# Moving blocks in and out of the inverse's layout: 32x32 transposes on VectorE in place of a trip through DRAM, and the first chunk inverted by itself

## The chip, the core and the metric

The kernel runs on one core of a Trainium2 chip. The core has a matrix engine (PE, TensorE; its weight loads are shown apart as PEld), a vector engine (DVE, VectorE), an activation engine (ACT, ScalarE), a general engine (POOL, GpSimd) and a sequencer for transfers (SP, SyncE). Each engine takes its instructions in the order of its own queue and waits on semaphores for the others. Transfers (DMA) are issued from the queues of SP, ACT and POOL. SBUF is the on-chip memory of 128 partitions, PSUM the accumulator memory that PE writes to. The metric is the device time of one execution in microseconds, as the median of several runs.

## The reference

A linear attention with the delta rule, and behind it a feed-forward block with LayerNorm. Four batches of eight heads, 768 tokens, head size 48; model width 384, hidden width 1536, all in fp32 (the feed-forward weights arrive as float64).

```python
k_n = k / (np.linalg.norm(k, axis=-1, keepdims=True) + 1e-06)
for t in range(S):
    y[:, :, t] = np.einsum('bhd,bhde->bhe', q[:, :, t], state)
    v_old = np.einsum('bhde,bhd->bhe', state, kt)
    state = state + bt[:, :, :, None] * np.einsum('bhd,bhe->bhde', kt, vt - v_old)
...
xn = (x - mu) / np.sqrt(var + 1e-06) * g_ln        # x: heads side by side, B x S x 384
ch = np.maximum(xn @ w_ch1, 0.0) @ w_ch2
return (x + ch)
```

## The kernel before, in words

The recurrence over tokens is cut into twelve chunks of C = 64 tokens. Inside a chunk the tokens' dependence on each other is a triangular system for each head. Its matrix comes from the Gram matrix K K^T of the chunk (64x64 for each of the 32 heads), scaled by beta and the norms. The kernel inverts that triangle, and then every chunk is a handful of matmuls: `recur` (L570) forms `p_k` and `p_y` from the running state, `p_u` with the inverse, the state's update `p_s`, and the output. The layout of the Gram matrices is: 64 tokens of one batch group on partitions 0 to 63, of the other group on 64 to 127, then 16 heads and 64 columns in the free dimension (`gsb`, 128 x 16 x 64).

The inverse (`inverse`, L443) works in another layout: one partition holds one diagonal block of one head, as L x L elements in its free dimension, so that DVE eliminates 128 blocks at once with L-1 pairs of small instructions (L475 multiplies, L480 subtracts). Chunks come in slabs of SLAB = 2. For the later slabs L is BK = 32: 2 chunks x 2 groups x 2 blocks x 16 heads are the 128 partitions (`blocks`, L402). For the first four chunks L is FB = 16 (`first_blocks`, L422), two chunks side by side in the free dimension. To get from one layout to the other, the kernel writes `gsb` to a DRAM tile `gd` (L389, L371), gathers blocks from there with eight or sixteen DMAs into `gb` (L406, L432), inverts, writes the result `xb` to a DRAM tile `xd` (L484), and scatters it with as many DMAs into `xt` (L414, L438), which has the Gram's layout again and was zeroed at the start (L258). After that `first_join` (L520) puts 16-blocks together to 32-blocks, and `join` (L492) 32-blocks to 64, each with a DVE transpose, two sets of small matmuls (`p_e`, `p_z`) and copies.

The feed-forward block of a chunk (`ffn`, L649) has 36 matmuls into `p_h`, evicted by ACT (`h_f`, L660), and 24 into `p_o`, evicted by DVE with the residual. Each matmul call leaves two records in the profile. The weights arrive as pairs of 32-bit words (float64) in twelve pieces of 768 KB into two buffers (`words`, L204) and are decoded to fp32 by `to_fp32` (L267): one ACT instruction (L277) and five DVE instructions (L279 to L294). Pieces 0 to 5 are the first matrix, 6 to 11 the second.

The order of the work: everything up to the `u` of chunk 0 stands in a block `in_this_order` (L686), which fixes the order of its instructions on each engine as written. The rest is written by a `Plan` (L24), whose due times (in units of its own) say in what order pieces are emitted; from there a scheduler gives each engine the earliest emitted instruction that it holds to be ready. `issue_after(ins)` keeps what is emitted within it behind `ins` on `ins`'s engine, and does not touch other engines. Before the change it is used with the last DVE instruction of the ordered block (`after`), for the weight pieces (L299) and the preparation of chunks 2 and 3, and in `queries` (L740) with the last gather on SP.

PSUM pools: `att` two buffers, `two` one buffer (shared by `p_g`, `p_k`, `p_u`, `p_s`), `by` one, `ffn` two (`p_h` and `p_o`).

Of the kernel before, what the change touches and what calls it, by code (L numbers as in the profile page):

```python
# [66 lines left out]

def in_turn(*gens):
    for gen in gens:
        yield from gen  # L70
# [3 lines left out]
def kernel(  # L74
# [10 lines left out]
):  # L85

# [29 lines left out]
    dram = ctx.enter_context(tc.tile_pool(name="dram", bufs=2, space=bass.MemoryType.DRAM))  # L116
# [94 lines left out]
    def places():  # L211

        for cc in range(SLAB):
            for e in range(2):
                for i in range(2):
                    yield ((cc * 2 + e) * 2 + i) * GH, cc, e, i
# [12 lines left out]
    with nc.allow_non_contiguous_dma(reason="short rows of g_ln"):  # L229
        load_beta_f(range(2), nc.gpsimd)  # L230
        nc.gpsimd.dma_start(out=g_sb, in_=g_ln.rearrange("(t p) -> p t", p=128))

# [10 lines left out]
    make_identity(nc, ident)  # L243
    umask = const.tile([128, 128], FP32, name="umask")
# [12 lines left out]
    for t in xts:  # L257
        nc.gpsimd.memset(t, 0.0)  # L258
# [40 lines left out]
    def weights(i0, i1, after=None, fetch=True):  # L299
        for i in range(i0, i1):  # L300
            with tc.issue_after(after) if after else nullcontext():
                to_fp32(i)
            if fetch:
                fetch_words()
            yield


    made, grams, deep_pools = {}, {}, []
    N_PREP = 4

    def turned(c, n):

        nc.vector.transpose(  # L313
            made[c][0][:, :, n].rearrange("p i (u t) -> p i u t", t=32), tblocks[(2 * c + n) % NTB]
        )

    def products(c, g, n0, n1):
# [10 lines left out]
        if n0 == 0:  # L328
            nc.scalar.copy(grams[c][0][:, heads].rearrange("p (j n) t -> p n j t", n=2), p_g[:, :, :, 0])  # L329
# [8 lines left out]

    def norms(c):
        ksum = work.tile([128, GH], FP32, name="ksum")  # L340
        for g in range(2):
            heads = slice(g * H, (g + 1) * H)
            ksq = work.tile([128, H, D], FP32, name="ksq", bufs=1)
# [12 lines left out]
    def new_chunk(c):  # L356
        gsb = work.tile([128, GH, C], FP32, name="gsb", bufs=4)
        gd = dram.tile([128, GH, C], FP32, name="gd", bufs=2 * SLAB)
        grams[c] = (gsb, gd)
# [3 lines left out]
    def prep(c):  # L363
# [7 lines left out]
        nc.sync.dma_start(out=grams[c][1], in_=grams[c][0])  # L371

    def prep_v(c):
# [3 lines left out]
        with tc.issue_after(after) if c < 4 else nullcontext():  # L377
            scale_v(c, norms(c), nc.gpsimd)
        yield

    def prep_g(c):

        new_chunk(c)
        with tc.issue_after(after) if c >= SLAB else nullcontext():
            turned(c, 0)
        for g in range(2):
            products(c, g, 0, 1)
            yield
        nc.sync.dma_start(out=grams[c][1], in_=grams[c][0])  # L389
# [10 lines left out]
    N_BLOCKS = 3 + BK // 2  # L400

    def blocks(m, engs):  # L402
        def gather(gb):
            for n, (p0, cc, e, i) in enumerate(places()):
                r0 = e * C + i * BK
                engs[n % len(engs)].dma_start(  # L406
                    out=gb[p0 : p0 + GH, 0],
                    in_=grams[SLAB * m + cc][1][r0 : r0 + BK, :, i * BK : (i + 1) * BK].rearrange("s h t -> h s t"),
                )

        def scatter(xd):
            for n, (p0, cc, e, i) in enumerate(places()):
                r0 = e * C + i * BK
                engs[n % len(engs)].dma_start(  # L414
                    out=xts[(SLAB * m + cc) % NXT][r0 : r0 + BK, :, i * BK : (i + 1) * BK],
                    in_=xd[p0 : p0 + GH, 0].rearrange("h s t -> s h t"),
                )
# [3 lines left out]
    def first_blocks(m, engs):  # L421

        def spots():
            for c in range(2):
                for e in range(2):
                    for b in range(C // FB):
                        p0 = (e * (C // FB) + b) * GH
                        yield p0, c, slice(e * C + b * FB, e * C + (b + 1) * FB), slice(b * FB, (b + 1) * FB)

        def gather(gb):  # L430
            for n, (p0, c, rows, cols) in enumerate(spots()):
                engs[n % len(engs)].dma_start(  # L432
                    out=gb[p0 : p0 + GH, c], in_=grams[SLAB * m + c][1][rows, :, cols].rearrange("s h t -> h s t")
                )

        def scatter(xd):
            for n, (p0, c, rows, cols) in enumerate(spots()):
                engs[n % len(engs)].dma_start(  # L438
                    out=xts[SLAB * m + c][rows, :, cols], in_=xd[p0 : p0 + GH, c].rearrange("h s t -> s h t")
                )  # L440

        return inverse(2, FB, beta_f[:, SLAB * m : SLAB * m + SLAB], gather, scatter)

    def inverse(nb, L, beta_l, gather, scatter):

        def square(pool, name, **kw):
            return pool.tile([128, BK * BK], FP32, name=name, **kw)[:, 0 : nb * L * L].rearrange(
                "p (b s t) -> p b s t", b=nb, s=L
            )
# [4 lines left out]
        gb = square(blk, "gb")  # L454
# [9 lines left out]
        xb = square(blk, "xb")  # L464
# [3 lines left out]
        nc.gpsimd.memset(xb, 0.0)  # L468
        nc.gpsimd.tensor_copy(out=diagonal(xb), in_=db)
# [13 lines left out]
        xd = square(dram, f"xd{L}")  # L483
        nc.sync.dma_start(out=xd, in_=xb)  # L484
        yield
        scatter(xd)
# [5 lines left out]
    def join(chunks):  # L492

        last = None
        for c in chunks:
            xt, gsb = xts[c % NXT], grams.pop(c)[0]
            xn = work.tile([128, GH, BK], FP32, name="xn", bufs=1)
# [22 lines left out]
    def first_join(c):  # L520

        xt, gsb = xts[c], grams[c][0]
        xn = blk.tile([128, GH, C], FP32, name="xn", tag="gb")
        nc.vector.transpose(xn, xt)
        quarters = [(slice(BK * n, BK * n + BK), BK * (n % 2)) for n in range(4)]
        p_e = ps_att([128, GH, FB], "p_e")
        for h in range(GH):
            for q, c0 in quarters:
                nc.tensor.matmul(p_e[q, h], gsb[q, h, c0 : c0 + BK], xn[q, h, c0 : c0 + FB])
        es = work.tile([128, GH, BK], FP32, name="es", bufs=1)[:, :, 0:FB]  # L530
        nc.scalar.mul(es, p_e, -1.0)
        yield
        p_z = ps_att([128, GH, FB], "p_z")
        for h in range(GH):
            for q, c0 in quarters:
                nc.tensor.matmul(p_z[q.start : q.start + FB, h], es[q, h], xt[q, h, c0 + FB : c0 + BK])
        for n, (q, c0) in enumerate(quarters):
            rows = slice(q.start, q.start + FB)
            copy = nc.vector.tensor_copy if n % 2 else nc.scalar.copy
            copy(out=xt[rows, :, c0 + FB : c0 + BK], in_=p_z[rows])  # L540
# [145 lines left out]
    with in_this_order(tc) as last:  # L686
        for c in two:
            for _ in prep_g(c):
                pass
        nc.vector.tensor_copy(out=scale_w[:, 0, 0:KC], in_=g_sb)  # L690
        nc.vector.tensor_scalar_mul(scale_w[:, 1, 0:KC], g_sb, 2.0**-52)
        for _ in weights(0, 1, fetch=False):
            pass
        inv = first_blocks(0, (nc.sync, nc.scalar))
# [4 lines left out]
        fetch_words()  # L699
        for _ in range(FB // 2):  # L700
            next(inv)
        knrm = norms(0)
        turned(0, 1)
        products(0, 0, 1, 2)
        for _ in inv:
            pass
        load_blocks(q, 1, 1, (nc.sync,))
# [116 lines left out]
```

## Time and profile before

| | |
|---|---|
| median of nine runs | 647.85 us (644.04 to 651.42) |
| the profiled execution's own time | 650.49 us |
| its span in the profile | 648.7 us |
| busy in the span: PE, DVE, ACT, POOL | 554.5, 328.6, 149.9, 124.0 us |
| DMA | 48.60 MB in 170980 packets, 164096 of them under 512 B |
| write of `gd`, one gather into `gb`, one scatter into `xt` (slabs of 32-blocks), issue to landing | 4.5, 3.5, 2.6 us |
| transfer of one piece of weights, 768 KB | 6.2 us |
| first FFN matmul (`p_h`) | at 90.6 us |

A line of a group of instructions reads: line of the kernel, engine, operation, written tile <- read tiles, shapes, count | busy us, mean ns of one | idle time of the engine just before them and what ended it. The chain of work that ended last is followed back from the end; its lines give start, length and what was running, "issue" being time for which the profile shows no wait. A waits line reads: who waited <- for whom: us in total, times, longest.

### The profile page before, as it was taken

To read this page: it belongs to the slowest core of one execution; us is meant where nothing else is said; L and a number is where in the kernel's file an instruction comes from. 1 tells how busy PE (TensorE), PEld (TensorE's weight loads), DVE (VectorE), ACT (ScalarE), POOL (GpSimd) and SP (SyncE) were. 2 spreads that over 40 slices of the span, in tenths; PEclk is the share of its full clock that TensorE was granted. 3 is DMA by queue.
4 is the path that set the end of the run, shared out by engine and by line. 5 is a ranking of instruction groups with operands and counts; after the bars stand their busy time and mean duration, and the time that the engine had idled before them with its cause. 6 is when DMAs were issued, how large, how long until landed. Compare 5 with 4: busy or idle time off the path is not lost.

```text
span 648.7 us, 19538 instructions
## 1 busy us (share of the span) xinstructions
PE 554.5 (85%) x8744; PEld 411.0 (63%) x8744; DVE 328.6 (51%) x683; ACT 149.9 (23%) x344; POOL 124.0 (19%) x197
## 2 busy tenths in 40 slices
PE   2016796875999979999989999799999799999997
PEld 2015684553786756786865877667868568777683
DVE  2453778998443994426982427953148722212000
ACT  2111332212231212232222221213312113213120
POOL 8042332015503222032310103020011000010100
PEclk9999998987999989899998999899999799999999
DMA  6775279547339304448215351141320020010101
GB/s 125 149 140 96 67 181 189 168 118 105 60 89 141 64 15 96 90 90 132 38 40 100 76 106 25 26 103 48 75 54 14 25 55 15 2 26 1 25 1 24
DMA packets 170980, 48.60 MB, mean 75 GB/s; under 512 B 164096, under 2 KB 165072, under 8 KB 170896
## 3 DMA queue, kind: packets, MB, share of 16 engines
q1 hardware_dynamic: 155760, 29.10, 24.5%
q0 software_dynamic: 6560, 17.72, 11.1%
q10 hardware_dynamic: 8576, 0.53, 0.9%
q8 instruction: 68, 1.11, 0.8%
q14 instruction: 16, 0.13, 0.1%
HBM read 33.69 MB, written 13.63 MB: 73 GB/s over the span
## 4 chain that ended last, share of the span: by engine, by line
PE 66%; DVE 12%; DMA 8%; issue 7%; ACT 3%; POOL 2%; SPq 2%; DVEq 0%; POOLq 0%; ACTq 0%
PE p_o L666 27%; PE p_h L655 22%; DVE tmp L475 4%; PE p_g L326 3%; DVE xb L480 3%; DMA words<-in_moe_w_ch_dram 3%; PE p_y L616 2%; PE p_e L504 2%; PE p_s L608 2%; DMA gb<-gd 2%; PE p_z L547 2%; DMA xt<-xd 2%; PE p_u L596 1%; DMA tb<-in_q_dram 1%; PE p_n L642 1%
## 5 line engine op out<-in xcount | busy, mean ns | idle before, releaser
L655 PE MATMUL p_h<-xnt,w_sb 128*128 128x256 f32 x864 | 213.6, 401 | 21.3 <-ACT h_f L660 14.9
L666 PE MATMUL p_o<-w_sb,h_f 128*128 128x384 f32 x576 | 200.6, 499 | 3.9 <-DVE w_sb L294 3.9
L655 PEld LDWEIGHTS p_h<-xnt,w_sb 128*128 128x128 f32 x864 | 166.4, 198 | 52.0 <-ACT h_f L660 17.7
L666 PEld LDWEIGHTS p_o<-w_sb,h_f 128*128 128x128 f32 x576 | 108.2, 193 | 71.1 <-DVE w_sb L294 4.2
L660 ACT ACTIVATE h_f<-p_h 128x256 f32<-128x256 f32 x144 | 54.7, 382 | 172.4 <-PE p_h L655 172.1
L326 PE MATMUL p_g<-kqt 48*64 48x64 f32 (+1 forms) x1024 | 36.1, 283 | 41.5 <-DVE kqt L313 35.0
L675 POOL DMA_DIRECT2D out_dram<-o x44 | 23.8, 544 | 249.0 <-DVE o L673 159.7
L148 POOL DMA_DIRECT2D tb<-in_k_dram x80 | 53.1, 670 | 74.8 <-DVE kqt L313 61.0
L326 PEld LDWEIGHTS p_g<-kqt 48*64 48x64 f32 x1024 | 28.1, 162 | 51.6 <-issue 33.3
L475 DVE TENSOR_TENSOR tmp<-xb,gb 128x31 f32<-128x31 f32 (+20 forms) x154 | 55.2, 358 | 4.7
L480 DVE TENSOR_TENSOR xb<-xb,tmp 128x31 f32<-128x31 f32 (+20 forms) x154 | 50.9, 330 | 4.2
L673 DVE TENSOR_TENSOR o<-p_o,x_ln 128x384 f32<-128x384 f32 x24 | 13.4, 558 | 70.5 <-PE p_o L666 70.0
L333 DVE TENSOR_TENSOR pt<-p_g,pmask 128x512 f32<-128x512 f32 x24 | 16.5, 688 | 52.8 <-ACT gsb L329 47.9
L313 DVE STREAM_TRANSPOSE kqt<-tb 128x1024 f32<-128x1024 f32 x24 | 29.5, 1236 | 4.8 <-DMA tb<-in_k_dram 4.5
L552 DVE COPY xt<-p_z 32x512 f32<-32x512 f32 x24 | 16.4, 684 | 23.4 <-PE p_z L547 23.0
L512 ACT ACTIVATE es<-p_e 32x512 f32<-32x512 f32 x24 | 14.1, 588 | 47.0 <-PE p_e L504 33.8
L567 DVE COPY x_ln<-p_y 64x384 f32<-64x384 f32 x12 | 6.7, 559 | 34.3 <-ACT x_ln L566 34.3
L643 ACT COPY xnt<-p_n 128x384 f32<-128x384 f32 x24 | 10.5, 481 | 50.0 <-PE p_n L642 49.9
L611 DVE TENSOR_TENSOR s_all<-s_all,p_s 128x768 f32<-128x768 f32 x11 | 10.5, 954 | 21.2 <-PE p_s L608 21.2
L329 ACT COPY gsb<-p_g 128x512 f32<-128x512 f32 x24 | 14.1, 585 | 29.0 <-PE p_g L326 29.0
L547 PE MATMUL p_z<-xt,es 32*32 32x32 f32 x768 | 17.8, 201 | 3.3 <-issue 2.3
L567 DVE COPY u<-p_u 64x384 f32<-64x384 f32 x12 | 6.7, 559 | 26.6 <-ACT u L566 26.4
(79 smaller groups left out, 477.8 us busy)
## 6 DMA issues: line engine op xcount, KB each, us to landing
words<-in_moe_w_ch_dram POOLq DMA_DIRECT2D x12, 768.0 KB, 6.2
gd<-gsb SPq DMA_DIRECT2D x12, 512.0 KB, 4.5
k<-in_k_dram SPq DMA_DIRECT2D x24, 192.0 KB, 3.8
v_raw<-in_v_dram SPq DMA_DIRECT2D x24, 192.0 KB, 4.1
out_dram<-o POOLq DMA_DIRECT2D x44, 96.0 KB, 2.5
tb<-in_q_dram SPq DMA_DIRECT2D x48, 64.0 KB, 2.8
tb<-in_k_dram POOLq DMA_DIRECT2D x40, 64.0 KB, 3.1
gb<-gd SPq DMA_DIRECT2D x32, 64.0 KB, 3.5
```

What stands on the lines that cost most here:

```text
L148: engs[m % len(engs)].dma_start(out=dst[p0 : p0 + 32, :, u, 0:w], in_=src[:, hp::2, toks, 32 * m : 32 * m + w].rearrange("b j t d -> t (b ...
L313: nc.vector.transpose(made[c][0][:, :, n].rearrange("p i (u t) -> p i u t", t=32), tblocks[(2 * c + n) % NTB])
L326: nc.tensor.matmul(p_g[toks, hp, j, n0:n1], kqt[rows, i, 0], kqt[rows, i, n0:n1])
L333: nc.vector.tensor_tensor(out=pt.rearrange("p (j n) t -> p n j t", n=2), in0=p_g[:, :, :, 1], in1=pmask[:, None, None, :].to_broadcast([12 ...
L475: nc.vector.tensor_tensor(out=t, in0=xb[:, :, 0:n, j : j + 1].to_broadcast([128, nb, n, w]), in1=gb[:, :, j : j + 1, j + 1 : L].to_broadca ...
L480: nc.vector.tensor_tensor(out=rest, in0=rest, in1=t, op=ALU.subtract)
L547: nc.tensor.matmul(p_z[r0, h], es[r1, h], xt[r1, h, BK:C])
L552: nc.vector.tensor_copy(out=xt[r0, :, BK:C], in_=p_z[r0])
L655: nc.tensor.matmul(p_h, w1_sb[:, t, f * 128 : (f + 1) * 128], xnt[:, t], start=(t == 0), stop=(t == KC - 1),)
L660: nc.scalar.activation(h_f, p_h, ACTF.Relu)
L666: nc.tensor.matmul(p_o, hs[f][:, g * 128 : (g + 1) * 128], w2_sb[:, f], start=(f == 0), stop=(f == FT - 1),)
L675: (nc.sync if c == NCH - 1 else nc.gpsimd).dma_start(out=out[2 * e + g, c * C : (c + 1) * C, :], in_=o[e * C : (e + 1) * C])
```

## The change

The DRAM tiles and all DMAs to and from them are gone. A 32x32 transpose on DVE takes a block's 32 token rows and 32 columns, which are chosen as (chunk, head) at a fixed column of the block, to 32 partitions that are (chunk, head) with the tokens in the free dimension. That is the layout of the inverse, if the partitions' order is group, block, chunk, head; `places` and with it the loading of `beta_b` follow. For 16-blocks a 32-row quadrant holds two blocks; there the transpose brings both to each partition, and two masks (`is_b`, sums over `ident`) select one. The way back is the same in reverse, into a tile `own` (`halves`), and `to_xt` spreads it into `xt` (the mask `is_u` zeroes the lower left block).

So that both diagonal blocks of a chunk are found in the same columns, rows 32 to 63 of each group keep their diagonal block in columns 0 to 31 of `gsb`. For the first four chunks a new `gram` computes only the upper triangle in that form; for later chunks `products` copies twice more. Chunk 0 is inverted alone, chunk 1 begins under chunk 0's joins and is finished in `second`; chunks 2 and 3 stay together. The first weight piece moves from ahead of the inverse to the end of the ordered block. `behind` applies `issue_after` with the last instruction of each engine.

```diff
+def behind(tc, last):
+    with ExitStack() as stack:
+        for ins in last.values():
+            stack.enter_context(tc.issue_after(ins))
+        yield
...
-                    yield ((cc * 2 + e) * 2 + i) * GH, cc, e, i
+                    yield ((e * 2 + i) * 2 + cc) * GH, cc, e, i
...
-    for t in xts:
-        nc.gpsimd.memset(t, 0.0)
+    nc.vector.tensor_reduce(
+        out=is_b, in_=ident.rearrange("p (q b s) -> p b q s", b=2, s=FB), axis=mybir.AxisListType.XY, op=ALU.add
+    )
...
-            with tc.issue_after(after) if after else nullcontext():
+            with behind(tc, after) if after else nullcontext():
                 to_fp32(i)
...
+    def gram(c):
+        kqt = made[c][0]
+        p_g = ps_two([128, 2, GH // 2, C], "p_g")
+        for j in range(GH // 2):
+            for u in range(2):
+                for hp, e in ((0, 0), (1, 1), (0, 1), (1, 0)):
+                    rows = slice(DP * hp, DP * hp + D)
+                    r0 = C * e + BK * u
+                    i = e * (GH // 2) + j
+                    nc.tensor.matmul(
+                        p_g[r0 : r0 + BK, hp, j, 0 : C - BK * u],
+                        kqt[rows, i, 0, BK * u : BK * u + BK], kqt[rows, i, 0, BK * u : C],
+                    )
+        dst = grams[c].rearrange("p (j n) t -> p n j t", n=2)
+        nc.scalar.copy(dst[:, :, :, 0:BK], p_g[:, :, :, 0:BK])
+        yield
+        for e in range(2):
+            rows = slice(C * e, C * e + BK)
+            nc.scalar.copy(dst[rows, :, :, BK:C], p_g[rows, :, :, BK:C])
...
         if n0 == 0:
-            nc.scalar.copy(grams[c][0][:, heads].rearrange("p (j n) t -> p n j t", n=2), p_g[:, :, :, 0])
+            dst = grams[c][:, heads].rearrange("p (j n) t -> p n j t", n=2)
+            nc.scalar.copy(dst, p_g[:, :, :, 0])
+            for e in range(2):
+                rows = slice(C * e + BK, C * e + C)
+                nc.scalar.copy(dst[rows, :, :, 0:BK], p_g[rows, :, :, 0, BK:C])
...
+    def to_xt(c, eng=None):
+        xt, own = xts[c % NXT], halves.pop(c)
+        if eng is None:
+            nc.scalar.mul(xt[:, :, 0:BK], own, is_u[:, 0:1])
+            nc.scalar.copy(xt[:, :, BK:C], own)
+        else:
+            eng.tensor_scalar(out=xt[:, :, 0:BK], in0=own, scalar1=is_u[:, 0:1], scalar2=None, op0=ALU.mult)
+            nc.scalar.copy(xt[:, :, BK:C], own)
+
+    def blocks(m):
         def gather(gb):
-            for n, (p0, cc, e, i) in enumerate(places()):
...
+            nc.vector.transpose(
+                gb[:, 0], pairs[m][:, :, :, 0:BK].rearrange("p c h s -> p s (c h)"),
+            )
+        def scatter(xb):
+            own = blk.tile([128, SLAB * GH, BK], FP32, name="own", tag="gb")
+            nc.vector.transpose(own.rearrange("p h t -> p t h"), xb[:, 0].rearrange("p s t -> p t s"))
+            for i in range(SLAB):
+                halves[SLAB * m + i] = own[:, i * GH : (i + 1) * GH]
+                to_xt(SLAB * m + i)
...
+    def first_blocks(chunks):
+        def gather(gb):
+            for n, c in enumerate(chunks):
+                tr = swapped("g_t").rearrange("p (s t) -> p s t", t=BK)
+                nc.vector.transpose(
+                    tr.rearrange("p s (b h) -> p s b h", b=2),
+                    grams[c][:, :, 0:BK].rearrange("p h (b s) -> p s b h", b=2),
+                )
+                nc.vector.tensor_scalar(
+                    out=gb[:, n], in0=tr[:, :, 0:FB], scalar1=is_b[:, 0:1], scalar2=None, op0=ALU.mult
+                )
+                nc.vector.scalar_tensor_tensor(
+                    out=gb[:, n], in0=tr[:, :, FB:], scalar=is_b[:, 1:2], in1=gb[:, n], op0=ALU.mult, op1=ALU.add
+                )
+        def scatter(xb):
+            own = blk.tile([128, len(chunks), GH, BK], FP32, name="own", tag="gb")
+            for n, c in enumerate(chunks):
+                xe = swapped("x_e").rearrange("p (b s t) -> p b s t", b=2, t=FB)
+                for b in range(2):
+                    nc.vector.tensor_scalar(
+                        out=xe[:, b], in0=xb[:, n], scalar1=is_b[:, b : b + 1], scalar2=None, op0=ALU.mult
+                    )
+                nc.vector.transpose(
+                    own[:, n].rearrange("p h (b t) -> p t b h", b=2), xe.rearrange("p b s t -> p t b s")
+                )
+                halves[c] = own[:, n]
...
-        nc.gpsimd.memset(xb, 0.0)
-        nc.gpsimd.tensor_copy(out=diagonal(xb), in_=db)
+        nc.vector.tensor_copy(out=diagonal(xb), in_=db)
...
     def first_join(c):
...
-        xn = blk.tile([128, GH, C], FP32, name="xn", tag="gb")
-        nc.vector.transpose(xn, xt)
+        xn = swapped("x_n").rearrange("p (h t) -> p h t", t=BK)
+        nc.vector.transpose(xn, own)
...
+        nc.gpsimd.memset(es[:, :, FB:], 0.0)
...
-            copy(out=xt[rows, :, c0 + FB : c0 + BK], in_=p_z[rows])
+        nc.vector.tensor_tensor(out=own[:, :, FB:], in0=own[:, :, FB:], in1=p_z, op=ALU.add)
...
         for c in two:
-            for _ in prep_g(c):
-                pass
...
-        for _ in weights(0, 1, fetch=False):
-            pass
-        inv = first_blocks(0, (nc.sync, nc.scalar))
+            new_chunk(c)
+            turned(c, 0)
+            first_grams.append(gram(c))
+            if c == 0:
+                next(first_grams[0])
+        inv, inv_1 = first_blocks((0,)), first_blocks((1,))
         next(inv)
         load_blocks(q, 0, 1, (nc.sync,))
         load_kv(0)
         next(inv)
+        for _ in first_grams[0]:
+            pass
+        for _ in first_grams[1]:
+            pass
         for _ in inv:
             pass
+        joining = first_join(0)
+        next(joining)
+        nc.vector.tensor_copy(out=scale_w[:, 0, 0:KC], in_=g_sb)
+        nc.vector.tensor_scalar_mul(scale_w[:, 1, 0:KC], g_sb, 2.0**-52)
+        next(inv_1)
+        next(joining)
+        to_xt(0, nc.vector)
+        joining = join((0,))
+        next(joining)
+        turned(0, 1)
...
+        knrm = norms(0)
+        for g in two:
+            products(0, g, 1, 2)
         scale_v(0, knrm, nc.vector)
+        for _ in joining:
             pass
+        next(inv_1)
         begin(0)
         recur_0 = recur(0)
         next(recur_0)
         next(recur_0)
+        for _ in weights(0, 1, fetch=True):
+            pass
         turned(1, 1)
...
-    after = last[mybir.EngineType.DVE]
+    after = last
     def second():
+        yield from inv_1
         joining = first_join(1)
...
     def queries():
-        gathers = [i for i in nc.cur_bb.bb.instructions if i.engine == mybir.EngineType.SP][-1]
-        with tc.issue_after(gathers):
...
-    plan.spread(second(), 7, 0, 12)
+    plan.spread(second(), 15, 0, 14)
```

## The prediction

> **What bounds the kernel now.** I read the stretches first, cut at 68.4 us, where chunk 0's `u` is complete, and at 158 us, where the last weight conversion (L294) ends. Columns: stretch, length, busy us of PE, PEld, DVE, ACT, POOL, granted clock, DMA share, GB/s.
>
> ```profile
> 0.00:68.40 68.40, 19.70 (x838) 17.53 (x838) 28.88 (x66) 11.49 (x21) 24.99 (x50) 1.00 0.65 121
> 68.40:120.00 51.60, 39.25 (x687) 31.64 (x675) 40.47 (x70) 15.59 (x33) 16.54 (x24) 0.93 0.75 174
> 120.00:158.00 38.00, 27.45 (x531) 17.64 (x535) 36.58 (x67) 9.87 (x19) 10.79 (x15) 0.92 0.47 103
> 158.00:649.00 491.00, 468.08 (x6719) 344.20 (x6711) 222.69 (x483) 112.98 (x272) 71.65 (x108) 0.97 0.29 56
> ```
>
> Three stages with three limits. Up to 68.4 no engine is half busy: a latency chain. From 68.4 to 158 DVE is busy 40.47+36.58 = 77.05 of 89.6 us and PE idles 22.9: DVE bounds, because FFN(0) waits for weights that DVE decodes. After 158 PE is busy 468 of 491: PE bounds, and what is gained earlier arrives at the end as it is.
>
> The chain of the first stage (start, us, what):
>
> ```profile
> 12.22 7.08 DMA words<-in_moe_w_ch_dram
> 19.39 4.13 DMA gb<-gd
> 23.55 1.95 DMA gb<-gd
> 25.51 2.26 DMA tb<-in_q_dram
> 30.23 10.39 issue
> 40.89 2.16 DMA xt<-xd
> 43.13 3.36 DMA xt<-xd
> 46.52 1.26 DVE xn L524
> ```
>
> The Gram blocks of chunks 0 and 1 are in SBUF at 14.9, but the inverse gets them at 27.8: 13 us for a write to DRAM and 16 gathers. ACT's eight gathers leave only at 19.39, because the weight scaling L277 is ahead of them in its queue and waits for `words`. The 10.39 of "issue" is the DVE loop (L475/L480, 30.1 to 38.7). From there to 46.5 the inverse goes out through `xd`: 8 us.
>
> For the second stage, the DVE groups between 68.4 and 158:
>
> ```profile
> L289 DVE SCALAR_TENSOR_TENSOR words<-words,scale_w 128x768 f32<-128x768 uint32 x11 | 11.1, 1008 | 0.1
> L279 DVE TENSOR_SCALAR top<-words 128x768 uint32<-128x768 uint32 x11 | 9.1, 824 | 3.3 <-ACT words L277 3.2
> L333 DVE TENSOR_TENSOR pt<-p_g,pmask 128x512 f32<-128x512 f32 x6 | 4.1, 686 | 3.5 <-PE p_g L326 3.4
> ```
>
> Eleven of twelve pieces are decoded here, with little waiting: work added to DVE here is nearly time. For the third stage, PE's waits after 160:
>
> ```profile
> PE p_h L655 <- ACT h_f L660: 12.7, 4, 4.3
> ```
>
> PE stalls only when ACT evicts `h_f` late. The 4.3 (to 233.5) is ACT standing behind its half of `u`, which waits for DVE, busy in an inverse. Prices:
>
> ```profile
> L498 DVE STREAM_TRANSPOSE xn<-xt 128x512 f32<-128x512 f32 x12 | 8.5, 707 | 10.0 <-PE p_e L504 5.1 <-DMA xt<-xd 4.9
> L465 DVE TENSOR_TENSOR gb<-gb,db 128x1024 f32<-128x1024 f32 x4 | 5.0, 1239 | 0.5 <-DVE db L463 0.4
> L344 ACT ACTIVATE ksq<-k 128x384 f32<-128x384 f32 x24 | 12.5, 522 | 8.4 <-DVE ksum L345 6.9 <-DMA k<-in_k_dram 1.3
> ```
>
> [...]one instruction can replace the DRAM trip; the trace has 0.71 us for 128x512 and 1.24 for 128x1024. [...](L286, tensor_scalar of 768: 0.55; L283, scalar_tensor_tensor of 768: 0.95). [...]The new transposes step 128 or 256 bytes; no transpose in this trace does, so 0.71 may be up to double (my bound).[...]
>
> **The change, first stage.** Removed: `gd`, the gathers, `xd`, the scatters, four 0.95 us memsets of `xt` on POOL, and the first weight piece ahead of the inverse. Estimated new chain, from 7.57 (first matmul, kept; k of chunk 0 arrives as before):
> - `gram(0)`: 128 records. L529 gave 15 ns a record, L326 35[...]: 1.9 to 4.5, take 3.3; copy 0.59: 11.6.
> - gather on DVE: transpose 0.71, tensor_scalar of 256 0.29 (0.15 + 256 at L286's rate), scalar_tensor_tensor of 256 0.42: 13.1.
> - norms to the loop, as now (27.78 to 30.10, less the halved L465): 15.1.
> - loop for one chunk: now 30 ops of 0.164 + 0.00097 per element (fitted to 0.19 at 30 and 0.29 at 128) with 0.036 between take 8.6; at half the elements 7.3: 22.4.
> - scatter 2x0.29 + 0.71: 23.8.
> - `first_join`: transpose 0.71, p_e 1.91, es 0.38, p_z 1.4, one add of 256 0.42 for four copies that now run one after another (54.48 to 56.14), handovers 0.4: 29.0. Chunk 1's gather (1.42) and `scale_w` (0.64) are queued on DVE ahead of the add, under p_e and p_z; uncovered they cost 2.
> - `to_xt` 0.6; join: transpose 0.71, p_e 1.92, es 1.2: 33.5. Ahead of p_z on PE and DVE now stand both Q products, norms, two `pt` and `scale_v`: PE reaches p_z at 36.9, DVE ends the copies at 40.1. Chunk 1's norms (1.5) hide under p_u.
> - p_u 2.1, unswap 1.6: 43.9. One PE pause such as the 2.15 at 51.1: 45.
>
> So `u` is ready at 45 in place of 68.4: 23.4 earlier. Costed at nothing here: `is_b` and `is_u` (two DVE reduces of 128 elements, some 0.3 each), before DVE's first transpose at 6.27, when it idles 2.85; the `xb` memset, on POOL before the gather; `es`'s new memset, on POOL under p_e; beta and g, issued behind `make_identity` (0.5), needed only at 14. Chunk 0's q, k and v loads on SP no longer stand behind gathers, so they land before 20 and are needed at 30. If one of these covers is missing it is half a microsecond each, the loads apart: late q would hold `turned(0,1)` and so both `pt` and p_z.
>
> **Second stage.** DVE gains: the first weight piece, formerly under the DMA wait, 0.56+0.96+0.56+1.02+1.02 = 4.1; chunk 1's own loop 30x0.164 + 1.3 = 6.2 and scatter 1.3; gather and scatter of chunks 2 and 3, 2x(1.42+1.3) + diagonal 0.2 = 5.6; chunk 1's xn transpose moved in 0.7; smaller joins -0.9. Sum 17.0: 77.05 becomes 94. Of the present idle 12.5 I keep 5:[...] chunk 1's loop fills waits. 94+5 = 99: weights done at 45+99 = 144 against 158, 14 gained. Bounds: no idle, 139 (19 gained); all idle kept, 151.5 (6.5); half-speed transposes take 3.8 more (seven of 0.53). The weight decode's ACT part now queues behind the head's last ACT instruction too; that takes it out of the way of `nrm` and `u`, and DVE's part waited there already. The third `words` fetch moves from 29.7 to after the first decode, about 49, and lands near 55 (6.2): the second piece (4.1) and chunk 1's loop (7.3) cover it on DVE; without them it is a wait of 6. The loads of `queries` are no longer held on SP behind the 16 gathers, so k's and q's blocks of chunks 2 and 3 come earlier.
>
> **Third stage.** Per later slab DVE gets two 128x1024 transposes and a diagonal copy, 2.7 in 90 us where it is at most 33.3 of 45 busy (285 to 330). ACT gets 32 extra Gram copies of 0.36 (the price of L540) and sixteen `to_xt` ops[...], under matmuls; but `to_xt` waits for a DVE transpose with `h_f` behind it. The removed DMAs were off PE's path. I take -2, half of one 4.3 stall, with 0 to 17 as bounds. `gram` of chunks 1 to 3 adds about 4 us of PE records in stages where PE idles 22.9 us: nothing, or up to 4 if they fall before an FFN matmul.
>
> **Sum.** 14-2 = 12: span 648.7 to 636.7, its execution 650.49 to 638.5. The median shown is 647.85, 2.6 below the profiled run, so 636 in medians.
>
> **Rivals.**
> - *Chain gain arrives nearly whole*: DVE's additions fall in its waits, and chunk 2's and 3's joins, no longer behind 13 us of scatter (140.3 to 155.8), move into PE's idle time. 19 + 3: 626. For: 22.9 us of PE idle. Against: the joins need DVE, the bound.
> - *DVE gives it back*: all 12.5 idle stays (it is waits on PE, ACT and words, not on the removed DMAs) and strided transposes run at half speed: 6.5-3.8-2: 647. For: 36.58 of 38 busy. Against: packets under 512 B were 164096 of 170980, many of them the removed ones.
> - *Slower, ACT's queue as the new wait*: each of four later slabs stalls PE as at 233, because `to_xt` stands before `h_f` until DVE has transposed. 4x4.3 = 17 against 14: 651; it decides from 14/4.3, more than three full stalls. Against: ACT is busy 113 of 491 there.
>
> **How the numbers follow.** Forecast 0.62 (its own range 630 to 642), whole gain 0.15, given back 0.14, slower 0.09. A change under 0.5% (3.2 us, 644.6 to 651.1) is about what a measurement of this kernel can't tell from none. Faster: 0.62+0.15 and half of the given-back case, 0.84; same 0.07, its other half; slower 0.09. 624 to 646 leaves out most of the last two cases, under 2 in 10.
>
> **What would show it.** Right: no `gd` or `xd` rows; the first L475 near 15; `u` (L566) near 44; last L294 near 144; DVE over 90% busy between; transposes of 0.71 and 1.24. Wrong: `u` after 50 (PE issue pauses, or q of chunk 0 late); transposes of 1.2 and 2.3; the weights not before 151; "PE p_h <- ACT h_f" above 20 us after the weights.

## The result and the profile after

The changed kernel takes 653.25 us in the median (18 runs, 651.27 to 657.07); the kernel before, on the same chips, 647.55 (55 runs). The ratio is 1.0106, interval 1.0085 to 1.0128: **slower by 1.1%**, where 636 was forecast. Ratios here and below leave out executions that took over 1.5% longer than the fastest one of the same kernel. The profiled execution took 654.85 us, its span is 653.1.

The first stage did what was forecast. The chain of the changed kernel, its first stage (start, us, what):

```profile
10.65 0.93 DVE g_t L478
12.00 0.50 DVE xb L485
21.46 0.63 DVE x_e L494 x2
22.11 1.08 DVE own L497
27.95 2.35 issue
39.46 1.87 PE p_z L603 x64
45.55 0.47 DVE u L623
```

No transfer stands between the Gram matrix and `u`; the loop starts at 14.24 and `u` of chunk 0 is complete at 46.5 instead of 68.4. Then nothing arrives at the end. The stretches of the changed kernel, cut there, at 92 us and at 165.2, where its last weight conversion ends (columns as in the prediction: length, busy us of PE, PEld, DVE, ACT, POOL, granted clock, DMA share, GB/s):

```profile
0.00:46.50 46.50, 17.28 (x770) 15.49 (x770) 29.13 (x86) 9.34 (x19) 15.54 (x38) 1.00 0.71 122
46.50:92.00 45.50, 31.48 (x908) 25.76 (x910) 36.62 (x79) 15.93 (x31) 13.78 (x21) 0.70 0.73 144
92.00:165.20 73.20, 56.03 (x1338) 39.32 (x1330) 61.07 (x112) 20.08 (x41) 24.46 (x32) 0.80 0.43 99
165.20:653.10 487.90, 459.38 (x5996) 334.25 (x5996) 219.72 (x482) 129.64 (x307) 64.35 (x101) 0.98 0.16 31
```

The kernel before at the same cuts:

```profile
0.00:46.50 46.50, 5.67 (x160) 4.76 (x160) 20.99 (x55) 7.99 (x13) 19.36 (x42) 1.00 0.71 139
46.50:92.00 45.50, 33.95 (x1211) 30.09 (x1212) 27.34 (x42) 11.73 (x24) 14.25 (x22) 1.00 0.53 110
92.00:165.20 73.20, 53.78 (x891) 36.18 (x889) 61.53 (x110) 18.34 (x38) 21.72 (x31) 0.88 0.69 145
```

PE's busy time times its granted clock is my estimate, a rough one, of its work in full-speed microseconds. At 46.5 the changed kernel has done 17.3 against 5.7: 11.6 us ahead. In the next stretch it does 31.48 x 0.70 = 22.0 against 34.0 and the lead is gone; at 165.2 it has done 84.1, the kernel before 87.0. PE is busy almost as long, but at a lower clock. That column was in the prediction's first view and I used it for nothing. In the eight kernels below that also invert chunk 0 by itself, the same stretch does 26 us of work, so 4 of the missing 12 us belong to this execution; by 165 most of the lead is gone in them too (e1: 90.3 of work against 87.0).

DVE's groups between 46.5 and 165.2 in the changed kernel:

```profile
L305 DVE SCALAR_TENSOR_TENSOR words<-words,scale_w 128x768 f32<-128x768 uint32 x12 | 12.1, 1008 | 0.1
L375 DVE TENSOR_TENSOR pt<-p_g,pmask 128x512 f32<-128x512 f32 x6 | 4.1, 685 | 2.9 <-PE p_g L364 2.7
L497 DVE STREAM_TRANSPOSE own<-x_e 128x512 f32<-128x512 f32 x3 | 3.3, 1085 | 0.0
L596 DVE TENSOR_TENSOR own<-own,p_z 128x256 f32<-128x256 f32 x3 | 1.3, 421 | 6.1 <-PE p_z L595 6.1
```

DVE works 97.7 us here, near the 94 forecast, but idles 21 of 118.7 us, not 5, and the largest item is a wait for PE's `p_z`. After the weights, PE's waits of the changed kernel from 160 on:

```profile
PE p_h L711 <- DVE o L729: 9.6, 4, 3.1
PE p_h L711 <- ACT h_f L716: 9.5, 5, 3.5
```

Before, there were 12.7 for `h_f` and none for `o`.

A small account serves all runs below. From the stretch view in rows of 1 us, for each profiled execution: PE's idle time (length less busy) and its clock loss (busy times one less the clock). What is left I call work. It should be equal but for the 256 records that the new `gram` has more, and comes out at 531 to 540 us, though no matmul record is missing (8744 with the old head, 9000 with the new one). One reason is that not every matmul takes twice as long where the clock is 0.50: a record of `p_k` in the changed kernel takes 218 ns at the shortest, and 303 to 340 from 100.4 to 102.4, at 0.50; one of `p_h` 379 at the shortest and up to 796. So a row is good to some us only, and it is one execution: that of the kernel before took 2.9 us more than its median. Idle + clock loss, us:

| kernel | 0 to 46.5 | 46.5 to 92 | 92 to 165 | 165 to the end |
|---|---|---|---|---|
| before | 41.4 + 0 | 11.1 + 0 | 19.2 + 5.9 | 22.5 + 9.7 |
| after | 29.3 + 0 | 13.9 + 9.3 | 17.0 + 12.9 | 28.7 + 10.2 |

Up to 165 us that is 77.6 before and 82.4 after; from there 32.2 and 38.9. (The eight other kernels with chunk 0 by itself have 75 to 79 up to 165.) So both halves must be explained: why a lead of 12 us is gone by 165, and why the later slabs got dearer.

### The profile page after: what moved, and what is told of

Read it like the earlier page. It is cut to its first block, busy times and chain, and to the rows that moved or that the text cites. A ratio compares the mean times of both kernels' runs of the same rounds, so it can differ in the third digit from the quotient of the medians.

```text
span 653.1 us, 19935 instructions
## 1 busy us (share of the span) xinstructions
PE 564.2 (86%) x9000; PEld 414.8 (64%) x9000; DVE 346.5 (53%) x756; ACT 175.0 (27%) x396; POOL 118.1 (18%) x192
## 4 chain that ended last, share of the span: by engine, by line
PE 54%; DVE 27%; issue 7%; ACT 7%; DMA 3%; POOL 1%; SPq 0%; ACTq 0%; DVEq 0%; POOLq 0%
PE p_h L711 23%; PE p_o L722 18%; DVE tmp L536 6%; DVE xb L541 6%; PE p_g L364 2%; ACT es L570 1%; ACT ksq L389 1%; PE p_e L562 1%; DVE own L466 1%; DVE ksum L390 1%; PE p_z L603 1%; PE p_k L641 1%; DVE gb L460 1%; PE p_u L652 1%; PE p_z L595 1%
## 5 line engine op out<-in xcount | busy, mean ns | idle before, releaser
L711 PE MATMUL p_h<-xnt,w_sb 128*128 128x256 f32 x864 | 217.4, 403 | 24.5 <-DVE o L729 9.6
L722 PE MATMUL p_o<-w_sb,h_f 128*128 128x384 f32 x576 | 205.2, 507 | 4.6 <-ACT h_f L716 2.6
L711 PEld LDWEIGHTS p_h<-xnt,w_sb 128*128 128x128 f32 x864 | 166.3, 199 | 57.4 <-ACT h_f L716 11.6
L722 PEld LDWEIGHTS p_o<-w_sb,h_f 128*128 128x128 f32 x576 | 109.9, 197 | 74.6 <-issue 5.7
L731 POOL DMA_DIRECT2D out_dram<-o x44 | 23.5, 538 | 315.9 <-DVE o L729 282.5
L541 DVE TENSOR_TENSOR xb<-xb,tmp 128x60 f32<-128x60 f32 (+24 forms) x169 | 52.0, 308 | 4.2
L536 DVE TENSOR_TENSOR tmp<-xb,gb 128x31 f32<-128x31 f32 (+15 forms) x124 | 42.1, 340 | 3.4
L329 DVE STREAM_TRANSPOSE kqt<-tb 128x1024 f32<-128x1024 f32 x24 | 29.3, 1229 | 4.4 <-DMA tb<-in_k_dram 2.6
L390 DVE TENSOR_REDUCE ksum<-ksq 128x8 f32<-128x384 f32 x24 | 13.1, 552 | 31.9 <-ACT ksq L389 31.7
L364 PE MATMUL p_g<-kqt 48*64 48x128 f32 (+1 forms) x768 | 26.9, 275 | 2.2 <-DVE pt L375 1.7
L364 PEld LDWEIGHTS p_g<-kqt 48*64 48x64 f32 x768 | 20.8, 147 | 12.1 <-issue 5.8
L652 PEld LDWEIGHTS p_u<-v_raw,xt 64*64 64x64 f32 x768 | 14.9, 151 | 8.4 <-issue 4.3
L652 PE MATMUL p_u<-v_raw,xt 64*64 64x48 f32 x768 | 17.0, 237 | 3.1 <-DVE v_raw L646 2.0
```

What stands on the lines that cost most here:

```text
L329: nc.vector.transpose(made[c][0][:, :, n].rearrange("p i (u t) -> p i u t", t=32), tblocks[(2 * c + n) % NTB])
L364: nc.tensor.matmul(p_g[toks, hp, j, n0:n1], kqt[rows, i, 0], kqt[rows, i, n0:n1])
L390: nc.vector.tensor_reduce(out=ksum[:, heads], in_=ksq, axis=mybir.AxisListType.X, op=ALU.add)
L536: nc.vector.tensor_tensor(out=t, in0=xb[:, :, 0:n, j : j + 1].to_broadcast([128, nb, n, w]), in1=gb[:, :, j : j + 1, j + 1 : L].to_broadca ...
L541: nc.vector.tensor_tensor(out=rest, in0=rest, in1=t, op=ALU.subtract)
L652: nc.tensor.matmul(p_u[half(e ^ hp), hp, j], xt[half(e), 2 * j + hp], vv[half(e), 2 * j + hp])
```

## The experiments

All times are medians; ratios are against runs of the kernel before on the same chip, with 95% intervals.

**First set: slabs or second stage.** Theory A: the loss lies in the later slabs, where DVE starts the inverse as soon as its gather is done, in the middle of other work. Theory B: it lies in the second stage, where the joins of chunks 2 and 3 hold up the weights on DVE.

e1_slab_dram: the changed kernel, later slabs through DRAM again, without the extra Gram copies.

```diff
     def blocks(m):
         def gather(gb):
-            nc.vector.transpose(gb[:, 0], pairs[m]...)
+            for p0, cc, e, i in places():
+                nc.sync.dma_start(out=gb[p0 : p0 + GH, 0], in_=gds[SLAB * m + cc]...)
         def scatter(xb):
-            nc.vector.transpose(own..., xb...)
-            ... to_xt(SLAB * m + i)
+            nc.sync.dma_start(out=xd, in_=xb[:, 0])
+            for p0, cc, e, i in places():
+                nc.sync.dma_start(out=xts[...]..., in_=xd[p0 : p0 + GH]...)
```

> The changed kernel's head and first four chunks, the later slabs (chunks 4 to 11) through DRAM again as before. Theory A (about 6 us are lost in the later slabs, because the inverse's DVE loop, no longer delayed by transfers, runs into the x_ln chain and the eviction of p_o): 647 us, and PE's waits for the eviction of p_o gone. Rival (the whole loss is in the second stage, the slabs cost nothing): 653, as the changed kernel.

Measured: 632.97 (631.03 to 635.38), ratio 0.9809 (0.9772 to 0.9846). The later slabs on DVE cost 20 us, more than any theory had. This version beats both kernels.

e2_slab_only: the kernel before with the later slabs on DVE and nothing else (the same edit the other way round).

> The kernel before with only the later slabs changed (transposes on DVE in place of DRAM). Theory A: 653 to 654, six over the kernel before, although nothing in the head differs. Rival (slabs cost nothing, the loss is the second stage's): 647 to 648.

Measured: 660.66, ratio 1.0239 (1.0191 to 1.0287): 15 us dearer. Theory A's direction holds, with more than twice its size.

e3_join_held: the changed kernel, the joins of chunks 2 and 3 held on DVE behind the last decoded weights.

```diff
-                yield from first_join(c)
+                joining = first_join(c)
+                with tc.issue_after(decoded[0]):
+                    next(joining)
```

> The changed kernel, with the joins of chunks 2 and 3 held on DVE behind the last decoded weight piece. Theory B (in the second stage these joins, ready sooner, tie DVE's queue to PE's and so delay the weights): last weight decoded before 155 us in place of 165, first o of FFN(0) before 160 in place of 168, 646 to 649 us in all. Rival (PE's halved clock and its pauses[...] set the second stage, wherever the joins stand): last weight at 162 or later, 652 to 654.

Measured: 655.0, ratio 1.0151 (1.0115 to 1.0188). The last weight conversion starts at 148.2 instead of 164.2, 16 us earlier, and the time doesn't fall at all. Theory B falls, and with it the yardstick of my second step: when the weights are ready doesn't by itself set the end.

e5_gather_late: the changed kernel, the slabs' gather held behind the DVE work due before it, 20.5 plan units later. No instruction is removed.

```diff
+            so_far = [i for i in nc.cur_bb.bb.instructions if i.engine == mybir.EngineType.DVE][-1]
+            with tc.issue_after(so_far):
                 nc.vector.transpose(...)
...
-            plan.spread(blocks(m), N_BLOCKS, times[1], times[2])
+            plan.spread(blocks(m), N_BLOCKS, times[1] + 20.5, times[2] + 8)
```

> The changed kernel, with the gather transpose of each later slab pinned on DVE behind the work due before it, 20.5 plan units later (behind xn_ln of an earlier chunk); no instruction is added or removed. Theory A (it is when the loop runs, not what it costs): 647 us. Rival (it is the price of the added instructions, transposes of 2 us and 32 more ACT copies): 653, unchanged.

Measured: 645.43, ratio 0.9997 (0.9973 to 1.0021): 8 us back by order alone. So this part of what the slabs cost isn't the price of their instructions.

**Second set: which part of the slabs.** e1 is taken apart.

f1_copies: e1 with the 32 extra Gram copies on ACT (nothing reads their result).

> The slabs through DRAM (633.0) plus the 32 extra Gram copies on ACT alone, whose result nothing reads here. Theory A, the loss lies in when DVE's instructions of the inverse start: the copies cost ACT 32 x 0.36 = 11.5 us under matmuls, time 633 to 636. Rival B, ACT's queue is the bound (the copies and to_xt stand before h_f): 640 to 645, the copies being half of what ACT got more.

f2_scatter_only: e1 with the way out on DVE and `to_xt` on ACT, gather through DRAM.

> Later slabs: gather through DRAM, no extra copies, only the way out of the block layout on DVE with to_xt on ACT. Theory A, the early start of the loop after a gather on DVE is what costs: 634 to 638, near the 633.0 of slabs wholly through DRAM. Rival B, to_xt waits in ACT's queue ahead of h_f: 643 to 650.

f3_gather_only: the changed kernel's gather and copies, the way out through DRAM.

> Later slabs: gather on DVE (with the extra copies), the way out through DRAM, no to_xt. Theory A, the loop starts as soon as the gather is done, between the instructions of the layer norm chain: 646 to 653, all or most of the loss. Rival B, to_xt in ACT's queue: 636 to 643.

Measured: f1 631.87 (0.9789, 0.9756 to 0.9822), f2 631.59 (0.9775, 0.9744 to 0.9807), f3 638.74 (0.9893, 0.9842 to 0.9944). Copies: nothing. Way out: nothing. Gather: 7 us. All of it together, the changed kernel: 20. Neither theory had that the two parts cost more together than apart. The traces show how, in one slab. The changed kernel in the third slab, DVE, PE and ACT by time (start, us, engine and line, what, idle before and what ended it):

```profile
402.85 0.55 DVE L729 TENSOR_TENSOR o<-p_o,x_ln 128x384 f32<-128x384 f32 x1
...
403.45 1.56 PE L711 MATMUL p_h<-xnt,w_sb 128*128 128x256 f32 x6 [3.12 <-DVE o L729]
...
414.01 4.25 PE L711 MATMUL p_h<-xnt,w_sb 128*128 128x256 f32 x12 [3.48 <-ACT h_f L716]
...
411.32 0.72 ACT L451 ACTIVATE xt<-own,is_u 128x512 f32<-128x512 f32 x1 [5.88 <-DVE own L466]
```

The gather on DVE is done at 379, so the loop is ready and is put ahead of the second `o`. DVE works through it without a pause and comes to `o` at 402.85, with PE waiting 3.12 for its PSUM buffer. Then the loop ends at 409, while PE is still in the `p_h` half of its chunk: ACT stands 5.88 us at `to_xt`, waiting for `own`, with `h_f` behind it, and PE waits another 3.48. The same place in f2:

```profile
390.32 0.56 DVE L734 TENSOR_TENSOR o<-p_o,x_ln 128x384 f32<-128x384 f32 x1 [3.41 <-PE p_o L727]
...
418.16 0.72 ACT L453 ACTIVATE xt<-own,is_u 128x512 f32<-128x512 f32 x1 [5.86 <-DVE own L471]
...
415.41 4.78 PE L727 MATMUL p_o<-w_sb,h_f 128*128 128x384 f32 x14
```

`o` is so early in DVE's order that DVE waits for PE. ACT stands at `to_xt` just as long, 5.86 us, but PE is in its `p_o` half and needs no `h_f`: free. And in f3 the early loop is over (400.98) before `u` is due, DVE waits for `u` and not the other way round, and nothing stands in ACT's queue: there is only the wait for `o`. PE's waits from 160 on, f3 and then f2:

```profile
PE p_h L716 <- DVE o L734: 11.0, 5, 3.1
```

```profile
PE p_h L716 <- ACT h_f L721: 6.9, 4, 2.6
```

f4_xt_late: e5, with `to_xt` given due times 8 and 4 units before its join.

> The changed kernel with the gather held late (645.4) and to_xt moved from right behind the transpose to 8 and 4 plan units before its join, so that ACT doesn't wait for DVE. Theory A, what is left of the loss is the price of the work itself: 643 to 646. Rival B, ACT stands at to_xt with h_f behind it: 635 to 640, PE waits for h_f falling from 16 to under 8 us.

Measured: 643.88, ratio 1.0005 (0.998 to 1.0029), no difference to e5. The trace says why: `to_xt` still runs right behind `own` (413.07 behind 410.91). The due time only sets the order of emission; the scheduler still took it first. The question needed a hard order:

h3_xt_last: the same, with `to_xt` within `issue_after` of the last ACT instruction emitted before it.

> The changed kernel with the gather held late and to_xt held on ACT behind the work due before it, that is behind the last h_f of the chunk. Theory, ACT's waits at to_xt with h_f behind them are the part that was left (2.2 us a slab and the clock after it): 632 to 638. Rival, what is left is the price of the work on DVE and ACT: 642 to 645.

Measured: 640.23, ratio 0.9903 (0.9875 to 0.9931). Below e5 and f4 by 0.9 to 1.0%, but above the 632 to 638 that I gave. PE's wait for `h_f` ahead of `p_o`, 4.4 us in e5, is gone; the waits for `h_f` ahead of `p_h` (10.1, from ACT standing at its half of `u`) and for `o` (4.6) stay. Order thus gives back 13 of the 20 us with every block still on DVE. The 7 that are left against e1 are about what PE waits more: h3, and then e1, from 160 on:

```profile
PE p_h L717 <- ACT h_f L722: 10.1, 4, 2.7
PE p_h L717 <- DVE o L735: 4.6, 5, 1.3
```

```profile
PE p_h L719 <- ACT h_f L724: 7.1, 4, 2.6
```

**Third set: where the rest came from.** e1 was 12 us faster than the kernel before, near the 14 that I had forecast for the first two stages. The account contradicts the reading that this is that gain: e1's loss up to 165 us is 76.7, that of the kernel before 77.6. Its 12 us lie in the slabs (20.4 against 32.2), though both send them through DRAM. In the kernel before, DVE's norms (`ksum`) of the next chunks stand inside a slab's loop, ahead of the copy of `u`; in e1 they don't, and there `ksq` shares a ring of two buffers with the join's `x_n`. Theory C: the ring's order did it. Rival D: the head.

h1_ring_only: the kernel before with that ring alone.

```diff
-            ksq = work.tile([128, H, D], FP32, name="ksq", bufs=1)
+            ksq = swapped("ksq")[:, 0 : H * D].rearrange("p (h d) -> p h d", d=D)
...
-            xn = work.tile([128, GH, BK], FP32, name="xn", bufs=1)
+            xn = swapped("x_n").rearrange("p (h t) -> p h t", t=BK)
```

> The kernel before, with one thing of the change alone: ksq and the join's xn take turns in one ring of two buffers, as in the changed kernel, in place of a buffer each. Blocks still go through DRAM and the head is the old one. Theory C, the ring keeps the norms (ksq on ACT, ksum on DVE) out of the later slabs' loops, where they hold up the copy of u and with it h_f: 631 to 636, so the 12 us that the slabs through DRAM won came from here. Rival D, they came from the new head: 643 to 647.

Measured: 645.53, ratio 1.0012 (0.9981 to 1.0044). The norms do leave the loop in slabs 3 and 4 and `u` is copied 2 us earlier (413.04 instead of 415.27 in the third slab), but that moves no time that can be measured. Theory C falls.

h4_two_together: f2 with chunks 0 and 1 inverted together in the head, as the kernel before does.

```diff
             first_grams.append(gram(c))
-            if c == 0:
-                next(first_grams[0])
-        inv, inv_1 = first_blocks((0,)), first_blocks((1,))
+            next(first_grams[c])
+            if c == 0:
+                next(first_grams[0], None)
+        inv, inv_1 = first_blocks((0, 1)), iter(())
```

> Chunks 0 and 1 inverted together in the head again, with gather and scatter on DVE, the later slabs gathered through DRAM (beside 631.6 with chunk 0 alone). Theory D, the head's gain counts: chunk 0's u comes 4 to 5 us later and the time grows by 3 to 5, 635 to 637. Rival C, the head's gain is given back before 165 us whatever its size, and chunk 1's loop is no longer among the weights: 629 to 633.

Measured: **620.42** (617.63 to 626.43), ratio 0.9604 (0.9564 to 0.9644), 11 us below f2 and the fastest kernel here. The two theories had 635 to 637 and 629 to 633. Chunk 0's `u` comes at 54.3, 8 us later than in the changed kernel, and the kernel is 11 us faster.

**Fourth set: is that so with the changed kernel itself?** Theory F: chunk 1's inverse among the weight conversions costs 11 us whatever the slabs do. Rival G: slabs on DVE take that back.

i2_after_two: the changed kernel with that one thing undone (the diff of h4).

> The changed kernel with one thing undone: chunks 0 and 1 are inverted together. Theory F, chunk 1's inverse among the weights costs 11 us whatever the slabs do: 640 to 645. Rival G, the slabs on VectorE take the lead back in stalls: 649 to 653.

Measured: 640.25 (637.98 to 641.61), ratio 0.9902 (0.9869 to 0.9934): 13 us below the changed kernel.

i3_chip_two: h3 with the same, no block through DRAM anywhere.

> Nothing through DRAM, chunks 0 and 1 inverted together, the slabs' gather held late and to_xt behind the chunk's last h_f (640.2 with chunk 0 alone). Theory F: 627 to 632. Rival G: 637 to 641.

Measured: 628.7, ratio 0.9735 (0.9697 to 0.9774), 11 us below h3 by the ratios. Three times out of three (h4, i2, i3) it is 11 to 13 us, as F has it. The stretches of i2, cut as above:

```profile
0.00:46.50 46.50, 13.76 (x676) 12.34 (x678) 27.75 (x72) 8.33 (x16) 15.68 (x37) 1.00 0.70 121
46.50:92.00 45.50, 35.53 (x1065) 30.50 (x1062) 35.42 (x57) 16.44 (x32) 13.92 (x22) 1.00 0.49 101
92.00:165.20 73.20, 58.10 (x1304) 40.67 (x1305) 60.63 (x115) 24.06 (x49) 29.33 (x42) 0.88 0.67 141
```

At 46.5 it is 3.5 us behind the changed kernel (13.8 of work), at 92 it is 10 ahead (35.5 at full clock against 22.0), at 165.2 it has done 100.4 against 84.1 (90.3 in e1). DVE is as busy as in the changed kernel, 35.4 and 60.6 us, and has got further: the last weight conversion starts at 154.0 instead of 164.2. Two things differ: DVE's order, and the amount of its work, since one loop of 30 instructions does for both chunks what two loops did (7.6 us of busy time in place of 12.1). In the changed kernel, DVE by time:

```profile
57.56 0.21 DVE L541 TENSOR_TENSOR xb<-xb,tmp 128x63 f32<-128x63 f32 x1
...
58.62 0.20 DVE L536 TENSOR_TENSOR tmp<-xb 128x60 f32<-128x60 f32 x1
58.75 1.00 DVE L310 SCALAR_TENSOR_TENSOR w_sb<-top,scale_w,words 128x768 f32<-128x768 f32 x1
59.68 0.21 DVE L541 TENSOR_TENSOR xb<-xb,tmp 128x60 f32<-128x60 f32 x1
...
84.16 0.42 DVE L596 TENSOR_TENSOR own<-own,p_z 128x256 f32<-128x256 f32 x1 [3.74 <-PE p_z L595]
```

The 0.2 us instructions of chunk 1's loop take turns with others of 0.5 to 1 us, mostly of the weights. The loop, a chain, ends at 67.0; 17 of its instructions lie in the last 19 us. In i2, with both chunks together, all 30 run from 18.75 to 27.4. So chunk 1's `p_z` is added at 84.16, in i2 already here:

```profile
55.64 0.42 DVE L596 TENSOR_TENSOR own<-own,p_z 128x256 f32<-128x256 f32 x1 [2.65 <-PE p_z L595]
```

In those 28 us PE is busy for 19.0, at a mean clock of 0.62 (0.50 from 54 to 67 and from 74 to 87), and a record of `p_h` takes up to 0.79 us (at 78.59) where the shortest takes 0.38. The first of the two stretches at 0.50 is in this execution alone, the second in all nine kernels that invert chunk 0 by itself. No run kept chunk 1 apart with its loop in one piece, so how much of the 11 to 13 us is the chain's late end and how much the 4.5 us less of work on DVE isn't separated; that the weights 16 us earlier gained nothing in e3 speaks for the chain.

i1_ring_diag: h1, and in the later slabs `xb` zeroed ahead of the gather and its diagonal copied by DVE, as in the changed kernel.

```diff
+        if L == BK:
+            xb = square(blk, "xb")
+            nc.gpsimd.memset(xb, 0.0)
         gb = square(blk, "gb")
         gather(gb)
...
-        nc.gpsimd.tensor_copy(out=diagonal(xb), in_=db)
+        nc.vector.tensor_copy(out=diagonal(xb), in_=db)
```

> The kernel before with the shared ring, and in the later slabs xb set to zero ahead of the gather and its diagonal copied by VectorE, as the changed kernel has them; blocks through DRAM, head as before. With the ring alone it was 645.5. Theory E, the rest of what the slabs through DRAM gained comes from these: the loop isn't held by POOL and VectorE's loop is 21.1 us instead of 23.0: 634 to 639. Rival, it comes from where the new head leaves the engines when the slabs begin: 643 to 646.

Measured: 638.79, ratio 0.9887 (0.9841 to 0.9932), by the ratio 7 us below the kernel before. At the upper end of theory E: with the ring, two small parts of the change that I had priced at a fraction of a microsecond gain 7 us, with the head and the DRAM trips of the kernel before. PE's wait for `h_f` from 160 on falls from 12.7 to 7.8 (11.0 in h1):

```profile
PE p_h L665 <- ACT h_f L670: 7.8, 4, 4.2
```

Theory E's second reason, the shorter loop, hardly explains it. The loop's own busy time in the last three slabs does fall, from 23.5, 22.2 and 22.4 to 21.1 or 21.2, but h1 has 22.4, 21.1 and 21.2 and gained nothing. Which of the two parts it is wasn't tried. The account from 165 on is 25.0, against 18.9 in f2; what makes the last 6 us of f2's slabs I haven't found. e1 and i1 share these parts and the DRAM trips of the later slabs, and differ in the main in the head and the first four chunks: 0.9809 and 0.9887 are some 5 us apart (the intervals allow 1 to 9). So not more than that is left of the 14 us forecast for the first two stages, and by the account it too lies behind 165 us (20.4 against 25.0), none of it ahead (76.7 against 75.5).

The account of the runs that settle it:

| kernel | up to 165 us | 165 to the end | median |
|---|---|---|---|
| before | 77.6 | 32.2 | 647.6 |
| after | 82.4 | 38.9 | 653.3 |
| e1, slabs through DRAM | 76.7 | 20.4 | 633.0 |
| i2, chunks 0 and 1 together | 64.8 | 34.1 | 640.3 |
| h4, both | 63.6 | 16.0 | 620.4 |

## Why the prediction was wrong

- **First stage** ("`u` is ready at 45 in place of 68.4"): right. 46.5, the loop's start at 14.24 for "near 15", a PE pause of 2.35 for the assumed 2.15.
- **Prices**: that the new transposes could take up to double was my estimate alone, and as a bound it held. They take 1.03 and 1.08 us (128x512) and 1.96 and 2.10 (128x1024), 1.5 to 1.7 times the 0.71 and 1.24 of those in the kernel before. For the five of them in the second stage (not seven) that is 1.8 us more, of no weight.
- **Second stage** ("DVE gains: ... chunk 1's own loop 6.2 and scatter 1.3", "I keep 5 ... chunk 1's loop fills waits", "weights done at 144"): this is the step that failed first: at most some 5 us came of 14 (e1 against i1). The work was 97.7 for 94; the idle time was 21 for 5; the weights were done at 165. Under it lie two errors. Chunk 1's loop was priced as DVE time, but it is a chain on which all of chunk 1's PE work hangs, and interleaved with conversions it ended at 67. Moving it back to the head costs chunk 0 some 8 us and gives 11 to 13 us (i2, h4, i3); the part in this of DVE's saved 4.5 us stays open. And I measured the stage by the weights: e3 has them 16 us earlier and isn't faster. Full-speed PE work done by then was the thing to count.
- **Third stage** ("I take -2, half of one 4.3 stall, with 0 to 17 as bounds"): the second step that failed, wrong in two directions: with the first two stages at some -5, the +7 in all leaves about +12 here. Slabs on DVE cost 15 to 20 us (e2, e1), where the sum had them at nothing because the work was under matmuls. The early gather alone is 7 (f3); of the 20, holding the gather gives back 8 (e5) and holding `to_xt` behind `h_f` another 5 (h3). The ring, the zeroing and the diagonal gain 7 (i1), which my sum doesn't contain. A stall was also priced at its wait alone, without the clock after it (12 records in 4.25 us for 2.86, behind the wait of 3.48).
- **Rivals.** "Slower, ACT's queue as the new wait" came nearest in time (651). Its mechanism is only a part: `to_xt` ahead of `h_f` is there, but PE's wait for `h_f` fell (12.7 to 9.5); the new wait is for `o`, on DVE; and of the 14 that the rival left to the first two stages at most some 5 came. "DVE gives it back" was right that the idle time of the second stage stays, and put too much on the half-speed transposes (3.8 for 1.8 us). Its ground, that work added to DVE is nearly time, holds nowhere in the slabs: f2 adds four transposes and sixteen `to_xt` at no cost, and e5 moves the time by 8 us without adding or removing one instruction.
- **What would show it**: "the weights not before 151" came (165), and "DVE over 90% busy between" failed (97.7 of 118.7, 82%); "`h_f` above 20" didn't come. The clock, which showed more than these, was not among the signs.

## What to carry to other kernels

A step that goes from a slow transfer to a fast instruction doesn't only lose a latency: the transfer had kept the work behind it back, and what is ready sooner is put sooner into the queue, ahead of instructions that other engines wait for (the same instructions in another order took 8 us less, e5). Ask of each such step what stands behind it now, and fix the order by hand if it matters. Cost a chain of small instructions by when it ends among its neighbours, not by the sum of its durations, and measure a stage by the work that the bounding engine has done at its full clock, not by one milestone alone.

## What was not expected of the hardware

A PE wait can cost more than its length. In the changed kernel the 12 records behind the 3.48 us wait take 4.25 us where they usually take 2.86, and in the kernel before, behind a wait of 3.35:

```profile
507.54 5.49 PE L655 MATMUL p_h<-xnt,w_sb 128*128 128x256 f32 x12 [3.35 <-ACT h_f L660]
```

The granted clock is 0.50 there for some 6.5 us, behind the other such waits of these two kernels for 3 to 4. It isn't each time: behind the 3.12 us wait above, 6 records take their usual 1.56. Behind the wait at the same place in f3, of 3.10, they take 2.93, and the clock is 0.50 for some 10 us:

```profile
394.67 2.93 PE L716 MATMUL p_h<-xnt,w_sb 128*128 128x256 f32 x6 [3.10 <-DVE o L734]
```

The clock of 0.50 comes behind shorter waits too: in the changed kernel the wait of 2.14 us that ends at 320.07 is followed by 0.50 for some 3 us, and in f2 one of 2.1 us (315 to 317) as well. The length alone doesn't decide it: the same wait of 2.43 us in the same slab passes without harm in e5 and is followed by a clock of 0.50 for some 3 us in f4 (e5, then f4):

```profile
408.06 2.86 PE L713 MATMUL p_h<-xnt,w_sb 128*128 128x256 f32 x12 [2.43 <-ACT h_f L718]
```

```profile
406.45 4.44 PE L712 MATMUL p_h<-xnt,w_sb 128*128 128x256 f32 x12 [2.43 <-ACT h_f L717]
```

In e5's profiled execution no wait after 170 us is longer than 2.7 us, and its clock is 1.00 from there on: as much waiting as in the changed kernel (11.7 + 4.4 + 4.1 against 9.6 + 9.5 us), in shorter pieces, at 8 us less. That the pieces' length is the reason is not shown: f4 has pieces no longer, loses 4.4 us to the clock from 165 on where e5 loses 1.2, and its median is no higher (643.88 against 645.43).
